# Another written-out issue order, with other banks and buffers, for attention followed by a gated FFN

## The chip, the cores and the metric

The kernel runs on one core of a Trainium2 chip. The metric is the device time of one execution in microseconds (us); the runs of one kernel are summed up by their median. The engines are called PE (TensorE), ACT (ScalarE), DVE (VectorE), POOL (GpSimd) and SP (SyncE, which only issues DMAs here).

## The reference

```python
k_proj = np.einsum('ks,bhsd->bhkd', E, k)
v_proj = np.einsum('ks,bhsd->bhkd', F, v)
scores = scale * np.matmul(q, k_proj.transpose(0, 1, 3, 2))
scores = scores - np.max(scores, axis=-1, keepdims=True)
attn = np.exp(scores)
attn = attn / (np.sum(attn, axis=-1, keepdims=True) + 1e-09)
x = np.matmul(attn, v_proj)            # then (B, H, S, D) -> (B*S, H*D)
gate = 1.0 / (1.0 + np.exp(-(x @ w_gate)))
out = (gate * (x @ w_val)) @ w_out
```

Attention has 8 batches, 8 heads, 1024 positions and 64 values to a head; E and F project the 1024 positions of K and V to 64. The FFN has 8192 tokens, 512 inputs, 1536 hidden values and 512 outputs. Inputs and output are float32; PE works in bf16.

## The kernel before

**The work.** A batch b goes through these stages. POOL loads K, V and q (`load_kv`, `load_q`, all through `load`, L559) and converts them to bf16 on the way. PE projects K and V (jobs `kv`). The projected K is transposed by a DMA of SP (`turnk`; on PE for batches 0 and 1), and so is q (`turnq`, `transpose_q`, L1491, DMA at L1494). A score job (`sc`) is four matmuls of 128 columns for 128 tokens and half of the heads. DVE takes the maximum (`top`) and subtracts it (`sub`; in some jobs PE subtracts, with the matrix `minus`), ACT takes the exponential (`exp`) into `pt`, which lies in the K half of the K and V buffer. SP transposes `pt` into `eT` (`turnp`, L1685, DMA at L1688). The products with V (`xo`, matmuls of 130 columns) give the sums too; DVE inverts them (`inv`), DVE or POOL divides (`div`, after a copy `ko` by ACT where POOL does it), and SP transposes the result into `xT` (`turnx`, L1748). Batch 0 is done by `first_batch`, with transposes on PE and its own job names (`pk`, `pv`, `tk`, `tq`, `xo0`, `tp`).

The FFN takes the 8192 tokens in 16 blocks of 512. Apart from the first block (`plain_steps`) and from the first and last output products (`o_plain`, jobs `Oplain`, 12 matmuls of 512 columns each), the products are made by a Strassen–Winograd scheme with seven products of halves instead of eight (`seven`, jobs `GA11`, `GS1`, `VS1`, `VA12`, `OA22` and so on, 4 to 6 matmuls of 256 columns each), with sums of the weights (`wsum`), of x and of the hidden values. ACT forms tanh(0.5 x) (`tanh`), and DVE forms (tanh + 1) times the value (`gate0`, L1067, and `hidden`, L1226); the factor 0.5 is applied when an output leaves PSUM. SP stores the output (`store`, L1309). While the FFN of batch p runs, the scores and products of batch p+1 and the loads and transposes of batch p+2 are placed between its matmuls.

**What sets the order.** The code makes 2923 jobs, each on one engine, numbered in the order in which the code creates them. The tuple `ORDER` (L159 to 315) names all of them once, in the order in which they are issued. `Scheduler.run` (L361) goes through it:

```python
assert sum(i >= 0 for i in ORDER) == len(self.jobs) and len(PLACES) == len(slots)
for s, p in zip(slots, PLACES):
    s.at = p
return [(lambda i=i: fill(-i)) if i < 0 else self.jobs[i].body for i in ORDER]
```

`Plan.emit` (L101) turns the list into one queue for each engine, which that engine works through in order. An instruction waits by semaphores for what it reads, and for the earlier users of what it overwrites; everything queued behind it on the engine waits too. So the place of a job in ORDER sets its place in its engine's queue only; what stands between two jobs of different engines tells how much work of the one engine lies between them. All loads but those of E and F are issued by POOL and all transposes and stores by SP, so ORDER sets the order of the DMAs as well.

A negative entry of ORDER is a filler (`busy`, L727): a matmul of the identity into bank 7, which keeps PE busy where its data is not there yet. −2 has 512 columns, −1 has 256. All fillers lie in the first hundred entries.

`PLACES` (L316 to 343) gives for each use of a PSUM bank one of 8 banks (`pF0` to `pF3`, `pA0` to `pA3`), and for each use of an SBUF scratch buffer one of 13 (two in the former place of E and F, the others in `spare`). Two uses of the same bank follow each other, with a wait where the first is not done.

**Numbers that come up later.** 0 to 15 are loads of weights and q, 30, 28, 31 and 29 transposes of q on PE, 38, 32, 58, 52 scores of batch 0 with what follows, 72, 79, 122, 125 its first `xo0` products, 128 to 183 the plain first block; 184 to 189 the loads of batch 1, 194 to 217 and 366, 367 weight sums and loads of `w_out`; 314 and 321 the projections of batch 1, 326 to 329 its `turnq`, 334 and 361 scores. Of `turnp`, 338, 347, 356, 365 are batch 1; 962, 971, 980, 989 batch 3; 1330 to 1357 batch 4; 1698 to 1725 batch 5; 2066 to 2093 batch 6. Of `turnx`, 391, 1013 and 2485; of `turnk`, 683, 1051, 1419. 424, 425; 1042, 1043; 1778, 1779 are pairs of q loads. The first readers of 338, 962, 980 and 1698 on PE are the `xo` jobs 368, 997, 1021 and 1733.

Of the kernel before, what the change touches and what calls it, by code (L numbers as in the profile page):

```python
# [153 lines left out]
class Job:  # L154
# [5 lines left out]
    16, -2, -2, -2, 17, 18, 0, 19, -2, -2, -2, -1, 28, 30, 29, 20, 3, 31, 21, -2, -2, -1, 22, 4, 38, 32, 1, 39,  # L160
    -2, -1, 23, 33, 2, 40, 24, 41, 9, -2, -2, 48, 25, 50, 42, 49, 5, 26, 34, 27, 51, 7, 35, 43, -2, -2, -1, 58,
    52, 8, 59, 46, 68, 36, 10, 60, 69, 61, 53, 6, 70, 37, -2, -1, 54, 11, 71, 62, 55, -2, -1, 44, 12, 75, 47,
    45, 14, 56, -2, -2, 72, 76, 15, 73, 63, 74, 13, 57, -2, -2, 66, 129, 77, 184, 64, 67, 135, 65, 78, 134, 189,
    79, 140, 80, 81, 194, 141, 128, 146, 188, 131, 136, 196, 148, 138, 142, 150, 195, 147, 144, 130, 143, 132,
    149, 197, 145, 137, 133, 84, 82, 366, 85, 157, 83, 198, 151, 86, 153, 87, 201, 92, 88, 102, 103, 93, 89,
    104, 156, 139, 160, 158, 94, 105, 152, 90, 95, 112, 96, 168, 91, 113, 106, 170, 172, 107, 154, 97, 114, 161,
    162, 108, 115, 180, 109, 116, 98, 182, 100, 110, 169, 117, 101, 174, 99, 181, 155, 122, 111, 171, 120, 123,
    173, 159, 124, 199, 163, 118, 121, 165, 119, 200, 183, 125, 218, 126, 127, 282, 367, 219, 210, 164, 190,
    283, 185, 203, 220, 191, 166, 187, 175, 284, 221, 234, 202, 186, 285, 298, 192, 193, 222, 299, 212, 321,
    167, 235, 223, 206, 236, 205, 322, 204, 225, 209, 323, 286, 237, 226, 300, 207, 324, 238, 301, 224, 325,  # L170
    211, 229, 239, 227, 266, 230, 250, 416, 267, 231, 251, 241, 213, 232, 287, 270, 254, 242, 417, 302, 255,
    252, 217, 303, 245, 418, 271, 257, 240, 246, 258, 273, 419, 253, 268, 274, 314, 243, 228, 269, 329, 256,
    315, 244, 247, 316, 272, 259, 328, 233, 289, 208, 317, 263, 216, 275, 261, 318, 326, 305, 264, 262, 279,
    306, 248, 277, 327, 265, 319, 280, 290, 176, 278, 320, 249, 177, 178, 281, 425, 361, 260, 179, 334, 352,
    309, 362, 444, 424, 335, 215, 336, 353, 337, 363, 330, 445, 339, 343, 331, 293, 447, 340, 294, 332, 344,
    333, 341, 364, 338, 214, 357, 345, 348, 450, 429, 354, 346, 349, 448, 355, 310, 449, 342, 358, 288, 347,
    350, 368, 375, 304, 276, 453, 369, 376, 552, 370, 377, 291, 371, 351, 451, 359, 356, 378, 292, 307, 380,
    360, 387, 558, 308, 454, 365, 559, 381, 388, 553, 382, 295, 560, 555, 455, 372, 554, 570, 389, 373, 390,
    384, 567, 374, 383, 385, 399, 379, 392, 386, 571, 393, 400, 557, 568, 401, 556, 394, 391, 311, 296, 569,
    395, 411, 396, 404, 312, 572, 297, 446, 402, 452, 412, 573, 313, 413, 428, 414, 408, 397, 405, 561, 574,  # L180
    398, 406, 409, 562, 403, 436, 407, 410, 576, 566, 437, 520, 564, 415, 577, 438, 521, 536, 456, 427, 439,
    537, 524, 575, 457, 522, 525, 540, 426, 565, 523, 538, 458, 539, 527, 563, 459, 440, 488, 578, 460, 489,
    423, 526, 442, 528, 579, 441, 421, 541, 529, 531, 492, 422, 532, 543, 530, 443, 580, 461, 533, 544, 581,
    420, 463, 493, 534, 462, 464, 490, 542, 465, 491, 472, 545, 467, 473, 469, 547, 495, 548, 476, 546, 549,
    477, 494, 470, 496, 479, 550, 468, 478, 480, 504, 497, 499, 481, 505, 474, 535, 787, 501, 508, 551, 483,
    509, 475, 690, 789, 511, 484, 485, 512, 510, 502, 500, 506, 486, 471, 706, 513, 466, 515, 430, 707, 487,
    498, 516, 691, 514, 503, 482, 694, 431, 517, 507, 695, 696, 786, 710, 432, 518, 697, 711, 433, 692, 790,
    698, 713, 434, 754, 699, 708, 582, 714, 519, 701, 693, 788, 703, 755, 717, 704, 702, 770, 435, 756, 718,
    674, 586, 771, 709, 758, 757, 590, 587, 604, 759, 774, 591, 772, 775, 792, 588, 705, 592, 761, 589, 617,
    773, 762, 793, 605, 595, 794, 765, 777, 606, 766, 801, 596, 593, 802, 778, 791, 594, 597, 607, 599, 722,  # L190
    600, 598, 608, 781, 584, 803, 601, 795, 583, 609, 806, 602, 618, 723, 807, 603, 782, 726, 808, 619, 613,
    724, 585, 727, 610, 677, 796, 620, 614, 611, 629, 810, 700, 615, 612, 712, 725, 760, 715, 616, 811, 630,
    763, 621, 631, 729, 812, 716, 626, 632, 641, 800, 738, 642, 627, 676, 622, 643, 719, 628, 739, 799, 638,
    623, 767, 720, 624, 634, 730, 740, 639, 635, 721, 644, 742, 636, 764, 646, 741, 625, 733, 743, 650, 640,
    776, 637, 647, 804, 768, 633, 648, 734, 779, 653, 797, 728, 769, 805, 654, 645, 651, 655, 652, 649, 783,
    809, 665, 658, 745, 798, 659, 731, 816, 660, 926, 746, 784, 735, 661, 666, 813, 785, 667, 662, 736, 749,
    888, 688, 737, 824, 686, 750, 744, 825, 814, 687, 889, 747, 689, 828, 663, 826, 815, 829, 892, 668, 780,
    827, 818, 890, 732, 817, 927, 656, 819, 893, 664, 904, 891, 895, 905, 831, 657, 751, 832, 840, 752, 896,
    669, 835, 841, 921, 908, 753, 899, 842, 748, 900, 844, 909, 920, 856, 836, 894, 922, 845, 911, 906, 857,
    925, 672, 897, 847, 912, 671, 858, 843, 848, 915, 898, 923, 670, 860, 916, 859, 851, 673, 820, 861, 872,  # L200
    907, 901, 928, 830, 852, 873, 929, 924, 862, 833, 930, 902, 863, 932, 935, 864, 910, 903, 675, 867, 934,
    874, 931, 936, 875, 938, 913, 933, 937, 876, 865, 917, 877, 837, 918, 868, 869, 822, 1058, 838, 879, 878,
    914, 880, 846, 870, 939, 919, 1059, 940, 849, 834, 941, 1155, 821, 853, 942, 883, 823, 866, 943, 1060, 680,
    850, 854, 881, 944, 681, 882, 1062, 884, 682, 885, 945, 1154, 839, 683, 1063, 947, 855, 1061, 1065, 886,
    679, 1064, 1066, 1158, 948, 684, 1067, 1122, 678, 871, 949, 1069, 1123, 1071, 887, 1070, 1074, 952, 1157,
    1124, 953, 1156, 1075, 1126, 685, 1159, 954, 1076, 1072, 946, 1078, 1077, 1125, 1160, 1043, 1079, 955, 1161,
    1127, 1042, 956, 958, 1162, 1081, 959, 963, 957, 967, 1129, 968, 1163, 1130, 964, 1164, 1073, 960, 1082,
    1169, 1165, 965, 961, 1080, 969, 966, 1085, 962, 1083, 972, 970, 976, 1133, 973, 1168, 951, 1138, 1134, 977,
    950, 1087, 1139, 971, 1170, 974, 1088, 1140, 975, 1142, 978, 1171, 1090, 1143, 1089, 1174, 1091, 1086, 981,
    1068, 1145, 1141, 997, 1175, 1146, 998, 982, 999, 990, 1149, 1176, 1000, 983, 1094, 979, 1092, 991, 1150,  # L210
    992, 980, 994, 1106, 1093, 995, 993, 985, 996, 1095, 1002, 1178, 1044, 1003, 1107, 986, 1167, 1009, 1179,
    1004, 1010, 987, 1011, 1128, 1001, 984, 1084, 1012, 1006, 988, 1097, 1007, 1180, 1108, 1008, 989, 1144,
    1098, 1005, 1131, 1021, 1018, 1110, 1109, 1166, 1096, 1013, 1022, 1147, 1101, 1023, 1111, 1135, 1019, 1099,
    1014, 1151, 1136, 1103, 1015, 1172, 1152, 1016, 1020, 1113, 1017, 1033, 1104, 1030, 1114, 1173, 1024, 1102,
    1026, 1256, 1177, 1025, 1117, 1257, 1034, 1054, 1181, 1027, 1055, 1028, 1182, 1031, 1184, 1137, 1057, 1046,
    1192, 1132, 1153, 1260, 1035, 1029, 1183, 1258, 1193, 1185, 1272, 1032, 1261, 1045, 1036, 1194, 1056, 1273,
    1196, 1195, 1208, 1037, 1259, 1263, 1209, 1274, 1112, 1197, 1186, 1275, 1276, 1187, 1105, 1115, 1199, 1198,
    1148, 1200, 1212, 1264, 1118, 1119, 1277, 1210, 1289, 1120, 1213, 1294, 1041, 1100, 1279, 1121, 1039, 1203,
    1201, 1215, 1038, 1188, 1224, 1216, 1040, 1205, 1189, 1204, 1293, 1267, 1206, 1295, 1225, 1211, 1280, 1219,
    1268, 1116, 1240, 1283, 1296, 1190, 1228, 1284, 1262, 1229, 1288, 1226, 1241, 1297, 1291, 1265, 1231, 1220,  # L220
# [1697 lines left out]
```

## Time and profile before

| | us |
|---|---|
| runs shown: 517.05, 517.59, 518.25; median | 517.59 |
| the profiled execution, its own time | 517.73 |
| its span (first to last instruction in the profile) | 515.9 |
| PE busy | 510.7 (99%), granted clock 1.0 |
| DVE busy | 438.5 (85%) |
| ACT busy | 371.5 (72%) |
| POOL busy | 171.4 (33%) |
| end of the last matmul | 513.3 |

The profile comes from one execution; its own time lies 0.14 us above the median. Times inside it count from the start of the span. A line of the timeline gives start, duration, engine, line of the kernel, operation, what is written and read, how many instructions were joined in the line, and in brackets how long the engine stood idle before it and who released it. Matmuls overlap, and a line's duration includes the way through the array: the time that a matmul costs is the distance to the next start. For a DMA, the timeline shows the issue on SP or POOL; the chain of waits and the list of DMA issues show how long it took to land.

### The profile page before, as it was taken

To read this page: it belongs to the slowest core of one execution; us is meant where nothing else is said; L and a number is where in the kernel's file an instruction comes from. 1 tells how busy PE (TensorE), PEld (TensorE's weight loads), DVE (VectorE), ACT (ScalarE), POOL (GpSimd) and SP (SyncE) were. 2 spreads that over 40 slices of the span, in tenths; PEclk is the share of its full clock that TensorE was granted. 3 is DMA by queue.
4 is the path that set the end of the run, shared out by engine and by line. 5 is a ranking of instruction groups with operands and counts; after the bars stand their busy time and mean duration, and the time that the engine had idled before them with its cause. 6 is when DMAs were issued, how large, how long until landed. Compare 5 with 4: busy or idle time off the path is not lost.

```text
span 515.9 us, 12160 instructions
## 1 busy us (share of the span) xinstructions
PE 510.7 (99%) x4724; PEld 424.5 (82%) x4727; DVE 438.5 (85%) x849; ACT 371.5 (72%) x714; POOL 171.4 (33%) x199
## 2 busy tenths in 40 slices
PE   8999999999999999999999999999999999999997
PEld 4556858879988888888888899888998899888884
DVE  6869999599988998879987899988998899877781
ACT  1557956789885797777878677885878678785841
POOL 9965014600634225230364014350164301503020
PEclk9999999999999999999999999999999999999999
DMA  9999999946939598962759859893279947320104
GB/s 154 197 198 207 185 165 195 182 75 142 185 104 187 121 170 157 177 101 66 148 148 184 144 104 180 179 183 80 60 128 185 196 83 160 107 62 19 66 2 163
DMA packets 140570, 71.58 MB, mean 139 GB/s; under 512 B 97248, under 2 KB 132320, under 8 KB 140512
## 3 DMA queue, kind: packets, MB, share of 16 engines
q0 software_dynamic: 35952, 29.89, 38.6%
q1 hardware_dynamic: 104560, 40.91, 36.8%
q8 instruction: 37, 0.61, 0.5%
q14 instruction: 21, 0.17, 0.1%
HBM read 60.29 MB, written 16.78 MB: 149 GB/s over the span
## 4 chain that ended last, share of the span: by engine, by line
PE 94%; DMA 3%; DVE 1%; ACT 1%; issue 0%; POOL 0%; POOLq 0%
PE pA L519 48%; PE pF L519 46%; DMA eT<-KVs 2%; DMA KVs<-in_k_dram 1%; DVE topf L1646 1%; ACT spare L533 0%; DVE pA L1673 0%; ACT KVs L533 0%; POOL KVs L560 0%; DVE hT L1067 0%; ACT EF L533 0%; DVE pF L1673 0%; ACT kpd L533 0%; ACT ost L533 0%; DVE wV L548 0%
## 5 line engine op out<-in xcount | busy, mean ns | idle before, releaser
L533 ACT ACTIVATE spare<-pF 128x512 f32<-128x512 f32 (+2 forms) x160 | 90.7, 578 | 39.2 <-PE pF L519 28.7
L533 ACT ACTIVATE spare<-pA 128x512 f32<-128x512 f32 (+2 forms) x157 | 88.7, 578 | 28.0 <-PE pA L519 19.3
L548 POOL TENSOR_TENSOR hT<-hT,hS 128x512 bf16<-128x512 bf16 x42 | 48.0, 1158 | 114.0 <-PE pF L519 48.8
L1226 DVE SCALAR_TENSOR_TENSOR hT<-spare,pA 128x512 bf16<-128x512 f32 x65 | 43.7, 678 | 10.2 <-PE pF L519 5.2
L1735 POOL TENSOR_TENSOR KVs<-spare,inv 128x384 bf16<-128x384 f32 (+1 forms) x44 | 33.2, 765 | 55.4 <-PE pF L519 27.8
L533 ACT ACTIVATE spare<-spare 128x512 f32<-128x512 f32 x77 | 47.6, 629 | 2.2 <-DVE spare L1157 2.2
L1157 DVE TENSOR_TENSOR spare<-pF,spare 128x512 f32<-128x512 f32 x63 | 42.7, 682 | 5.3 <-PE pF L519 3.9
L519 PE MATMUL pA<-wO,hT 128*128 128x256 bf16 (+1 forms) x323 | 44.6, 280 | 0.1
L519 PE MATMUL pF<-wO,hT 128*128 128x256 bf16 (+1 forms) x286 | 43.8, 294 | 0.1
L519 PE MATMUL pA<-xT,wV 128*128 128x256 bf16 (+1 forms) x236 | 39.0, 287 | 0.0
L1157 DVE TENSOR_TENSOR spare<-pA,spare 128x512 f32<-128x512 f32 x52 | 35.3, 681 | 4.0 <-PE pA L519 3.1
L1226 DVE SCALAR_TENSOR_TENSOR hT<-spare,pF 128x512 bf16<-128x512 f32 x51 | 34.5, 678 | 2.7 <-PE pF L519 2.2
L519 PEld LDWEIGHTS pA<-wO,hT 128*128 128x128 bf16 x324 | 31.4, 98 | 6.1 <-issue 0.2
L519 PEld LDWEIGHTS pF<-wO,hT 128*128 128x128 bf16 x288 | 27.9, 98 | 9.1 <-ACT ost L533 0.2
L519 PE MATMUL pF<-xT,wG 128*128 128x256 bf16 (+1 forms) x208 | 34.5, 287 | 0.0
L519 PE MATMUL pA<-xT,wG 128*128 128x256 bf16 (+1 forms) x200 | 31.8, 283 | 0.0
L560 POOL DMA_DIRECT2D Qb<-in_q_dram x18 | 14.0, 784 | 49.0 <-DMA kpD<-kpd 19.1
L519 PE MATMUL pA<-xS,tG 128*128 128x256 bf16 x200 | 30.0, 273 | 0.0
L548 POOL TENSOR_TENSOR xS<-xT,xS 128x512 bf16<-128x512 bf16 x14 | 16.4, 1172 | 38.3 <-DVE xS L548 20.9
L519 PE MATMUL pF<-xS,wG 128*128 128x256 bf16 x192 | 28.6, 273 | 0.0
L519 PE MATMUL pA<-xS,tV 128*128 128x256 bf16 x192 | 28.6, 273 | 0.0
L519 PE MATMUL pF<-xS,wV 128*128 128x256 bf16 x192 | 28.3, 273 | 0.0
(185 smaller groups left out, 1315.8 us busy)
## 6 DMA issues: line engine op xcount, KB each, us to landing
out_dram<-ost SPq DMA_DIRECT2D x63, 256.0 KB, 2.4
KVs<-in_v_dram POOLq DMA_DIRECT2D x15, 512.0 KB, 10.6
KVs<-in_k_dram POOLq DMA_DIRECT2D x14, 512.0 KB, 9.0
Qb<-in_q_dram POOLq DMA_DIRECT2D x14, 512.0 KB, 9.4
wO<-in_moe_w_out_dram POOLq DMA_DIRECT2D x2, 768.0 KB, 15.7
KVs<-in_k_dram POOLq DMA_DIRECT2D x4, 256.0 KB, 7.3
Qb<-in_q_dram POOLq DMA_DIRECT2D x4, 256.0 KB, 11.2
wV<-in_moe_w_val_dram POOLq DMA_DIRECT2D x4, 256.0 KB, 17.2
```

The costliest lines, as they stand in the source:

```text
L519: lambda e: e.matmul(o, lhsT, rhs, **kw),
L533: lambda e: e.activation(o, i, func, scale=scale),
L548: fn = lambda e: e.tensor_tensor(o, a, b, op)
L560: add("POOL", lambda e: e.dma_start(o, i), r=r, w=w, dma=sem, cost=0.78, nbytes=nbytes)
L1157: lambda e: e.tensor_tensor(PB(b)[:, :] if stay else BF(s), PB(b)[:, :], BF(s), ALU.add),
L1226: lambda e: e.scalar_tensor_tensor(o, y.rearrange("p (j c) -> p j c", j=2), 1.0, x.rearrange("p (j c) -> p j c", j=2), ALU.add, ALU.mult,),
L1646: lambda e: e.tensor_reduce((top if by_pe(b, t, y) else topf)[:, n : n + 8], PB(bk)[:, :].rearrange("p (n k) -> p n k", n=8), mybir.AxisLi ...
L1735: fn = lambda e: e.tensor_tensor(xto.rearrange("p (g h d) -> p h g d", g=2, h=H)[:, hh[0] : hh[1], :, :], o[:, :, 0:DH].rearrange("p (h g) ...
```

## The change

`ORDER` and `PLACES` are replaced. The jobs, their instructions and all other code are the same. ORDER has 2949 entries instead of 2948: one more filler of 512 columns (20 instead of 19; the 6 of 256 stay). Of the 906 entries of PLACES, 800 differ. In the diff, the first lines of both lists are shown, the lines around 338, around 962 to 1021 and around 1698, and the first line of PLACES.

```diff
 ORDER = (
-    16, -2, -2, -2, 17, 18, 0, 19, -2, -2, -2, -1, 28, 30, 29, 20, 3, 31, 21, -2, -2, -1, 22, 4, 38, 32, 1, 39,
-    -2, -1, 23, 33, 2, 40, 24, 41, 9, -2, -2, 48, 25, 50, 42, 49, 5, 26, 34, 27, 51, 7, 35, 43, -2, -2, -1, 58,
-    52, 8, 59, 46, 68, 36, 10, 60, 69, 61, 53, 6, 70, 37, -2, -1, 54, 11, 71, 62, 55, -2, -1, 44, 12, 75, 47,
-    45, 14, 56, -2, -2, 72, 76, 15, 73, 63, 74, 13, 57, -2, -2, 66, 129, 77, 184, 64, 67, 135, 65, 78, 134, 189,
-    79, 140, 80, 81, 194, 141, 128, 146, 188, 131, 136, 196, 148, 138, 142, 150, 195, 147, 144, 130, 143, 132,
...
-    306, 248, 277, 327, 265, 319, 280, 290, 176, 278, 320, 249, 177, 178, 281, 425, 361, 260, 179, 334, 352,
-    309, 362, 444, 424, 335, 215, 336, 353, 337, 363, 330, 445, 339, 343, 331, 293, 447, 340, 294, 332, 344,
-    333, 341, 364, 338, 214, 357, 345, 348, 450, 429, 354, 346, 349, 448, 355, 310, 449, 342, 358, 288, 347,
-    350, 368, 375, 304, 276, 453, 369, 376, 552, 370, 377, 291, 371, 351, 451, 359, 356, 378, 292, 307, 380,
...
-    1124, 953, 1156, 1075, 1126, 685, 1159, 954, 1076, 1072, 946, 1078, 1077, 1125, 1160, 1043, 1079, 955, 1161,
-    1127, 1042, 956, 958, 1162, 1081, 959, 963, 957, 967, 1129, 968, 1163, 1130, 964, 1164, 1073, 960, 1082,
-    1169, 1165, 965, 961, 1080, 969, 966, 1085, 962, 1083, 972, 970, 976, 1133, 973, 1168, 951, 1138, 1134, 977,
-    950, 1087, 1139, 971, 1170, 974, 1088, 1140, 975, 1142, 978, 1171, 1090, 1143, 1089, 1174, 1091, 1086, 981,
-    1068, 1145, 1141, 997, 1175, 1146, 998, 982, 999, 990, 1149, 1176, 1000, 983, 1094, 979, 1092, 991, 1150,
-    992, 980, 994, 1106, 1093, 995, 993, 985, 996, 1095, 1002, 1178, 1044, 1003, 1107, 986, 1167, 1009, 1179,
-    1004, 1010, 987, 1011, 1128, 1001, 984, 1084, 1012, 1006, 988, 1097, 1007, 1180, 1108, 1008, 989, 1144,
-    1098, 1005, 1131, 1021, 1018, 1110, 1109, 1166, 1096, 1013, 1022, 1147, 1101, 1023, 1111, 1135, 1019, 1099,
...
-    1863, 1899, 1710, 1693, 1900, 1822, 1711, 1874, 1701, 1901, 1865, 1808, 1875, 1694, 1905, 1904, 1695, 1779,
-    1866, 1876, 1696, 1702, 1703, 1826, 1877, 1697, 1878, 1906, 1704, 1827, 1698, 1804, 1712, 1828, 1907, 1713,
...
-    1715, 1824, 1870, 1721, 1864, 1820, 1912, 1783, 1881, 1825, 1914, 1882, 1722, 1716, 1733, 1726, 1915, 1734,
...
-    1748, 1913, 1846, 1903, 1844, 1835, 1749, 1847, 1880, 1872, 1849, 1778, 1883, 1757, 1839, 1902, 1758, 1837,
...
+    16, -2, -2, -2, 17, 18, 0, 19, -2, -2, -2, -1, 30, 28, 31, 20, 1, 29, 21, -2, -2, -1, 22, 4, 38, 3, 32, 39,
+    -2, -1, 23, 2, 33, 40, 24, 5, 41, -2, 34, 48, 25, 50, 8, 42, 49, 26, 7, 27, 51, 35, 43, -2, -2, -2, -1, 58,
+    6, 59, -2, -1, 46, 9, 52, 47, 68, 36, 10, 60, 69, 53, 61, 11, 37, 70, -2, 54, 75, 12, 55, 62, 44, 71, 13,
+    45, 56, 14, -2, -2, -2, -1, 72, 76, 74, 15, 63, 73, 57, -2, -2, 66, 129, 77, 64, 67, 135, 65, 78, 134, 79,
+    147, 80, 81, 194, 146, 140, 128, 142, 196, 141, 144, 143, 195, 136, 130, 131, 132, 197, 148, 133, 149, 150,
...
+    262, 319, 306, 216, 326, 249, 176, 320, 280, 177, 265, 278, 425, 178, 334, 281, 289, 309, 179, 361, 335,
+    352, 424, 343, 444, 336, 214, 337, 362, 290, 353, 363, 330, 445, 339, 293, 331, 447, 294, 340, 260, 332,
+    344, 333, 215, 338, 341, 348, 448, 450, 345, 342, 446, 349, 346, 310, 364, 347, 350, 276, 304, 451, 288,
+    354, 351, 357, 368, 375, 358, 355, 453, 369, 376, 356, 552, 370, 377, 291, 378, 429, 307, 292, 371, 359,
...
+    1126, 1075, 1124, 954, 945, 955, 1076, 887, 946, 1078, 1125, 956, 1160, 950, 1043, 1079, 953, 1067, 963,
+    957, 1161, 1042, 964, 1127, 958, 1077, 1071, 1162, 1129, 965, 967, 1130, 1163, 959, 1081, 1072, 1164, 968,
+    1082, 972, 966, 960, 1167, 1169, 1073, 969, 1133, 1168, 1080, 973, 961, 1138, 1083, 970, 976, 962, 1170,
+    974, 1139, 1087, 977, 975, 971, 1142, 1088, 1171, 1140, 1068, 1085, 978, 1134, 981, 1089, 1174, 1143, 1141,
+    1090, 997, 1175, 1091, 998, 1086, 999, 1145, 979, 982, 990, 1000, 1106, 1146, 980, 994, 983, 1092, 1176,
+    1149, 995, 991, 992, 1178, 951, 1150, 984, 993, 1094, 1093, 996, 985, 1095, 1002, 1009, 986, 1179, 1001,
+    1107, 1010, 1003, 1097, 987, 1004, 1128, 1084, 988, 1006, 1108, 1007, 1011, 1110, 989, 1098, 1008, 1012,
+    1021, 1144, 1180, 1131, 1096, 1005, 1111, 1022, 1109, 1172, 1023, 1147, 1014, 1024, 1013, 1018, 1113, 1019,
...
+    1893, 1817, 1859, 1895, 1801, 1420, 1685, 1860, 1802, 1894, 1680, 1689, 1421, 1688, 1623, 1778, 1805, 1861,
+    1690, 1708, 1779, 1806, 1691, 1800, 1818, 1896, 1692, 1681, 1709, 1693, 1821, 1803, 1897, 1822, 1807, 1898,
...
+    1703, 1904, 1865, 1700, 1876, 1697, 1826, 1701, 1809, 1698, 1905, 1877, 1702, 1712, 1704, 1878, 1827, 1906,
+    1713, 1866, 1816, 1705, 1907, 1828, 1819, 1706, 1869, 1714, 1829, 1830, 1707, 1733, 1879, 1823, 1820, 1715,
...
 PLACES = (
-    0, 3, 4, 2, 1, 2, 6, 1, 5, 0, 2, 0, 0, 1, 4, 3, 3, 2, 5, 0, 1, 0, 2, 1, 1, 5, 5, 0, 0, 8, 1, 10, 4, 2, 4, 2,
...
+    0, 3, 4, 2, 2, 1, 6, 1, 5, 0, 4, 4, 0, 1, 0, 3, 3, 2, 5, 4, 1, 1, 4, 2, 2, 5, 5, 2, 2, 8, 0, 9, 3, 7, 5, 7,
...
```

318 rows, old and new, of tables (ORDER, PLACES) are left out of this document.

## The prediction

> **What bounds the kernel now.** I read the page from its top: busy shares, the chain that ended last, then PE by stages, then the waits of PE, and at each wait the timeline around it.
>
> ```profile
> PE 510.7 (99%) x4724; PEld 424.5 (82%) x4727; DVE 438.5 (85%) x849; ACT 371.5 (72%) x714; POOL 171.4 (33%) x199
> ...
> q8 instruction: 37, 0.61, 0.5%
> ...
> PE 94%; DMA 3%; DVE 1%; ACT 1%; issue 0%; POOL 0%; POOLq 0%
> ```
>
> PE is busy 99% of the span and is 94% of the chain. Busy does not prove full speed, so I look at the step of a matmul. The chain has runs of PE work with nothing between:
>
> ```profile
> 57.56 1.31 PE pA L519 x12
> ```
>
> 12 matmuls of 256 columns in 1.31 us is 109 ns each; in the same way 512 columns take 216 ns, 130 columns 59, 128 columns 56. Priced with these steps, all PE work from the first K projection (7.50 us) on is 499.6 us. The work is fixed, so the list can win only what PE stands still between 7.50 and its last matmul (513.3 us). The stages show where that is:
>
> ```profile
> core 0: us, PE busy (x) PEld busy (x) DVE busy (x) ACT busy (x) POOL busy (x), PEclk, DMA share, GB/s
> 0.00:22.00 22.00, 19.93 (x163) 10.22 (x163) 16.27 (x51) 7.58 (x14) 20.87 (x32) 1.00 1.18 172
> ...
> 65.92:200.00 134.08, 133.61 (x1257) 112.87 (x1258) 120.09 (x233) 100.85 (x197) 44.18 (x50) 1.00 0.84 153
> 200.00:350.00 150.00, 150.00 (x1434) 132.17 (x1432) 131.62 (x250) 116.10 (x224) 50.26 (x57) 1.00 0.80 147
> ```
>
> The granted clock is 1.00 throughout. After 22 us almost nothing is left. Going through PE's rows and subtracting the step of each matmul from the distance to the next, I find 1.66 us of standing after 22 us that another order could remove: 0.16 at 22.6, and some 1.5 after 66 us. The two largest are these:
>
> ```profile
> 72.66 1.23 SPq L1688 DMA_TRANSPOSE eT<-KVs  x1
> ...
> 74.00 1.91 SPq L1494 DMA_TRANSPOSE qT<-Qb  x1
> ...
> 76.34 0.60 PE L519 MATMUL pA<-xS,wG 128*128 128x256 bf16 x4
> ...
> 77.14 0.35 PE L519 MATMUL pF<-vpD,eT 128*128 128x130 bf16 x3 [0.19 <-DMA eT<-KVs]
> ```
>
> Four steps of 109 ns from 76.34 end at 76.78; the `xo` product (job 368) starts at 77.14, so PE stood 0.36 us. It waited for the transpose of exponentials that SP issued at 72.66 (job 338). The chain shows how long that and a later one (980) took:
>
> ```profile
> 72.66 4.43 DMA eT<-KVs
> ...
> 191.90 4.82 DMA eT<-KVs
> ```
>
> The reader of 980 (job 1021) came 0.34 us late. The reader of 962 (997) came 0.07 us late, behind a transpose of 5.58 us. About 0.7 us is in pieces of 0.04 to 0.17 us behind ACT and DVE. So at most 1.6 us (0.3%) can be won; nothing bounds a loss.
>
> **What a transpose needs.** All 90 transposes of SP have an issue and a landing in the trace. The 59 with no load from POOL and no packet of PE's instruction fetch (queue q8, 37 of them, one for about 250 PE instructions, 12 to 13 us apart, 0.96 us each) beside them take 3.0 to 3.75 us, median 3.20. The 26 with such a fetch beside them have a median of 4.2, the 5 with a load alone 4.49; 18 of 90 are over 4.0. Against that stands what I call the cover: the PE work that ORDER lists between a transpose and its first reader. An issue comes 0.39 us ahead of its listed place in the median (5th percentile 1.2 ahead, 95th 0.48 behind). A reader waits, then, by about (duration − 0.39 − cover), where positive.
>
> **The change, part by part.** The same instructions stand in another order, with other banks and buffers, and one more filler of 512 columns on PE.
>
> *Start, to 22 us.* The weight loads are issued in another order. I lined up the new PE queue with the measured durations: the first `sub` product keeps 18.82, the ten products after it and the fillers follow without a gap, and the first `xo0` product that before had at 24.18 would start at 23.83, 0.35 us earlier; the 0.16 at 22.6 goes, one filler (0.216) is added. Every weight in my line-up lands at least 0.5 us ahead of its use.
>
> *The wall at 62 to 66 us.* The first scores of batch 1 need q transposed:
>
> ```profile
> 59.61 6.46 SPq L1494 DMA_TRANSPOSE qT<-Qb  x4
> ...
> 65.92 0.39 PE L519 MATMUL pF<-kpD,qT 128*128 128x128 bf16 x4
> ```
>
> The last q load ends a queue of loads that never runs dry from 21 to 62 us (2.5 us for each 512 KB). The new list puts the same bytes ahead of it, so I keep its landings: the two transposes needed first land at 63.4 and 65.3. Before, the reader came 0.60 us after that. In the new list the first reader (334) has 0.22 us less PE work ahead of it (54.64 instead of 54.86, fillers counted), and the start does this work 0.57 sooner (0.35 earlier, with 0.216 of filler more behind it): 65.92 − 0.22 − 0.57 = 65.13, so it waits to 65.35. Work after it is 445.16 us instead of 444.73. From before's 65.92 + 444.73 = 510.65 to 65.35 + 445.16 = 510.51: **−0.14** is all that the start leaves. Bounds: −0.35 if q lands earlier; +0.5 if the loads end 0.6 us later (a quarter of one 512 KB load).
>
> *338.* Cover 3.48 (two scores 0.45, an output product 2.59, one Strassen product 0.44) becomes 3.91 (one Strassen product more). Also 424, a q load beside it, is listed 2.4 us of PE work earlier. At 4.43 the wait would shrink by 0.43, more than its 0.36; a fetch near it leaves some chance of a longer one. **−0.30**, bounds −0.36 and +0.3.
>
> *980.* Cover 4.37 becomes 5.24, so 4.82 fits: **−0.34**, bounds −0.34 and 0.
>
> *962.* Cover 5.04 becomes 3.72: two scores and two products now stand ahead of it. The q loads 1043 and 1042 are listed where they were (167.5 and 168.4 us of PE work; before 167.8 and 168.4) and landed, before, at 172.9 and 176.4 on the same scale; 962 is listed at 173.9, so most of it still lies beside the second one. By the median with a load, 4.49 − 0.39 − 3.72 = 0.38, and its 0.07 of before goes: **+0.31**; bounds −0.07 (at 3.2) and +1.40 (at the 5.58 of before).
>
> *1698 and the short covers.* The new list has 14 transposes with cover under 4.0 (338, 347, 356, 391, 683, 962, 1013, 1051, 1357, 1348, 1419, 1698, 2075, 2485; least 3.05 and 3.28), the old list 8. At 3.2 none of them waits. 1698 (3.72) has two q loads moved ahead of it (listed 8.3 and 7.4 us before it; a q load lands 6 to 9 us after issue): **+0.10**, bounds 0 and 0.4. I place the fetches by the number of PE instructions, as in the trace; of the other twelve only 338 and 347 stand near one. So they get 0; the bound is the rival below.
>
> *Waits on ACT and DVE.* By PE distance 78 readers had under 0.3 us of margin and 76 have it now; under 1 us 358 and 340. **0**, bounds −0.5 and +0.5.
>
> *Ending.* After the last matmul one copy and one store, 2.6 us, in both; the last jobs lined up show no gap: **0**.
>
> Sum: −0.14 − 0.30 − 0.34 + 0.31 + 0.10 = −0.37. The profiled execution took 517.73 (span 515.9); 517.73 − 0.37 = 517.36. It lies 0.14 above the median of 517.59, so the forecast is **517.2**.
>
> **Rivals.**
> (a) *Nearly all waits go.* Start as above (−0.14), 338, 980 and 962 without wait (−0.36, −0.34, −0.07) and the pieces behind ACT and DVE too (some −0.7): −1.5, with 1698's +0.10 kept −1.4: **516.2**. For it: each wait can be removed by distance alone. Against it: the counts of narrow margins hardly fall.
>
> (b) *Covers decide nothing.* If what makes a transpose long is not its neighbours in time but happens to the ones that PE waits for, moves give and cost nothing: only the −0.14 stays, **517.45**. Against: 3.20 without neighbours, 4.2 and 4.49 with them. The Trainium skill, "Runtime: NRT & Kernel Launch", section "Instruction fetch mechanics", says that instructions are refilled in blocks of 256 and that crossing such a border is "mostly hidden". Its block agrees with a fetch for about 250 instructions here; for PE's own queue no row shows a stop at a fetch, but the transposes beside one are 1 us longer, which that sentence does not mention; by it, the transposes near a fetch would need no more cover than others and this rival's time would hold.
>
> (c) *The short covers run late; slower.* If the 14 lie beside a load, a store or a fetch more often than I place them, each waits by its duration − 0.39 − cover. At 4.2 their sum is 1.8 us, at 4.49 about 5.4; the old list's covers give 1.3 and 3.5 in the same way. The first three parts win 0.78; the lateness passes that and the 0.2% bound (1.03) together from 1.8 us on: 962's 0.31 and three more at 0.5 (a transpose of some 4.6). With four more at 0.5: 2.31 − 0.78 = +1.5 on the median, **519.1**. For it: 18 of 90 were over 4.0, which is 2.8 of 14 if my placing of fetches says nothing.
>
> (d) That the list does other work than before is excluded: same instructions but one filler.
>
> **How the numbers follow.** What can be told from no change is 0.2%, 1.03 us: faster is below 516.56, slower above 518.62. Forecast 0.42 (516.7 to 518.1), (a) 0.20, (b) 0.10, (c) 0.28. Faster 0.20 is (a); same 0.52 is the forecast with (b); slower 0.28 is (c). The range runs from (a) to a little over (c): 516.2 to 519.3, with a tenth left out at each end.
>
> **What would show it.** Right: no gap on PE ahead of 368 and 1021, one of 0.3 to 0.4 ahead of 997; the first scores of batch 1 start near 65.4; sum of PE's standing after 66 us 1.2 to 1.6. Wrong: scores later than 66 us (loads late, the wall moves everything), or several gaps of 0.3 to 1 ahead of `xo` products and of the first product of a block (readers of transposes), which is (c); or gaps of over 0.2 behind ACT and DVE, of which I expected none new.

## The result, and the profile after

| | before | after |
|---|---|---|
| median of 9 runs each | 517.59 | 519.42 |
| lowest and highest run | 516.98 to 519.26 | 518.62 to 520.38 |
| the profiled execution, its own time | 517.73 | 520.38 |
| its span | 515.9 | 518.6 |

The ratio is 1.0034, with a 95% interval of 1.0022 to 1.0047: the change makes the kernel slower by 1.83 us (0.34%). The profiled execution of after is the slowest of its nine runs, 0.96 above their median; so its trace shows where the time went, but more of it than the median has.

Page, parts 1 and 4, of after:

```profile
PE 510.4 (98%) x4725; PEld 424.3 (82%) x4728; DVE 438.6 (85%) x849; ACT 372.5 (72%) x714; POOL 170.6 (33%) x199
...
PE 93%; DMA 4%; DVE 2%; ACT 1%; issue 0%; POOL 0%; POOLq 0%
```

PE is busy as long as before, in a span that is 2.7 us longer. The work is the same; PE stands still more. The same stages as before show where (length, then busy time of PE, PEld, DVE, ACT, POOL, clock, DMA share, GB/s):

```profile
65.92:200.00 134.08, 132.93 (x1248) 112.38 (x1249) 118.07 (x231) 101.40 (x197) 41.41 (x50) 1.00 0.86 149
200.00:350.00 150.00, 148.28 (x1417) 130.18 (x1415) 129.91 (x246) 113.42 (x219) 51.30 (x58) 1.00 0.75 145
```

In the second stage before had no idle time of PE; after has 1.72 us. In the first it was 0.47 and is 1.15. The long transposes of the chain of waits are now three:

```profile
72.78 4.70 DMA eT<-KVs
...
185.27 5.10 DMA eT<-KVs
...
307.48 5.14 DMA eT<-KVs
```

They are 338, 962 and 1698. 980, long before, took 3.07. The timeline of PE at the readers of the last two, 997 and 1733:

```profile
188.96 0.61 PE L519 MATMUL pA<-xT,wG 128*128 128x256 bf16 x4
190.41 0.29 PE L519 MATMUL pA<-vpD,eT 128*128 128x130 bf16 x2 [0.84 <-DMA eT<-KVs]
...
310.90 0.60 PE L519 MATMUL pF<-xS,tG 128*128 128x256 bf16 x4
312.67 0.29 PE L519 MATMUL pF<-vpD,eT 128*128 128x130 bf16 x2 [1.16 <-DMA eT<-KVs]
```

Four steps of 109 ns after 188.96 end at 189.40, and 997 starts at 190.41: 1.01 us late. For 1733 it is 312.67 − 311.34 = 1.33. To see why the transposes landed late, look at what POOL had under way. The timeline of POOL, and the landings of its two loads of q (1043 and 1042) from issue, in us:

```profile
178.96 1.52 POOL L560 DMA_DIRECT2D Qb<-in_q_dram  x2 [13.98 <-DMA qT<-Qb]
...
DMA to landing us min/median/max: 6.9/8.0/9.0
```

The second load, issued at 179.74, lands at 188.74, and 962, issued at 185.27, at 190.37: 1.63 us after the load. 1698 was issued at 307.48, 7.5 us after the load 1779, which landed at 309.72; two stores ahead of 1698 in SP's queue landed at 310.13 and 310.78, and 1698 at 312.62.

The third loss is on DVE. Timelines of DVE, POOL and PE:

```profile
341.38 1.37 DVE L548 TENSOR_TENSOR xS<-xT 128x512 bf16<-128x512 bf16 x1
...
341.27 1.21 POOL L548 TENSOR_TENSOR hT<-hT,hS 128x512 bf16<-128x512 bf16 x1 [0.28 <-PE pF L519]
...
343.42 0.39 PE L519 MATMUL pF<-xS,wG 128*128 128x256 bf16 x2 [0.56 <-DVE spare L1157]
```

The sum 1924 on DVE (0.42 us in the trace of before) began 0.11 us after a sum of POOL (2035) and took 1.37, until 0.27 us after POOL's end. The sum `plusG` 1969 behind it came late, and the product 1973 that waits for it started 0.72 us late.

### The profile page after: what moved, and what is told of

Its sections match the earlier page's. It is cut to its first block, busy times and chain, and to the rows that moved or that the text cites. A ratio compares the mean times of both kernels' runs of the same rounds, so it can differ in the third digit from the quotient of the medians.

```text
span 518.6 us, 12152 instructions
## 1 busy us (share of the span) xinstructions
PE 510.4 (98%) x4725; PEld 424.3 (82%) x4728; DVE 438.6 (85%) x849; ACT 372.5 (72%) x714; POOL 170.6 (33%) x199
## 4 chain that ended last, share of the span: by engine, by line
PE 93%; DMA 4%; DVE 2%; ACT 1%; issue 0%; POOL 0%; POOLq 0%
PE pA L519 49%; PE pF L519 44%; DMA eT<-KVs 3%; DMA KVs<-in_k_dram 1%; DVE topf L1646 1%; DVE xS L548 0%; DVE pA L1673 0%; ACT KVs L533 0%; POOL KVs L560 0%; ACT ost L533 0%; DVE pF L1673 0%; DVE hT L1067 0%; ACT spare L533 0%; DVE spare L1157 0%; ACT EF L533 0%
## 5 line engine op out<-in xcount | busy, mean ns | idle before, releaser
L1735 POOL TENSOR_TENSOR KVs<-spare,inv 128x256 bf16<-128x256 f32 (+1 forms) x49 | 34.5, 715 | 84.3 <-ACT spare L533 25.2
L519 PE MATMUL pA<-wO,hT 128*128 128x256 bf16 (+1 forms) x383 | 55.3, 286 | 0.1
L1226 DVE SCALAR_TENSOR_TENSOR hT<-spare,pF 128x512 bf16<-128x512 f32 x65 | 43.6, 678 | 8.6 <-PE pF L519 6.5
L519 PE MATMUL pF<-xT,wV 128*128 128x256 bf16 (+1 forms) x244 | 38.9, 281 | 0.1
L1226 DVE SCALAR_TENSOR_TENSOR hT<-spare,pA 128x512 bf16<-128x512 f32 x48 | 32.4, 678 | 3.4 <-PE pA L519 2.3
L519 PE MATMUL pA<-wT,hS 128*128 128x256 bf16 x252 | 33.7, 273 | 0.0
L519 PE MATMUL pF<-wO,hT 128*128 128x256 bf16 (+1 forms) x226 | 32.9, 288 | 0.1
L519 PE MATMUL pF<-xS,tV 128*128 128x256 bf16 x216 | 32.4, 273 | 0.0
L519 PE MATMUL pA<-wT,hT 128*128 128x256 bf16 x240 | 31.7, 273 | 0.0
L533 ACT ACTIVATE EF<-pA 128x512 f32<-128x512 f32 (+2 forms) x33 | 18.7, 574 | 15.8 <-PE pA L519 14.3
```

The costliest lines, as they stand in the source:

```text
L519: lambda e: e.matmul(o, lhsT, rhs, **kw),
L533: lambda e: e.activation(o, i, func, scale=scale),
L1226: lambda e: e.scalar_tensor_tensor(o, y.rearrange("p (j c) -> p j c", j=2), 1.0, x.rearrange("p (j c) -> p j c", j=2), ALU.add, ALU.mult,),
L1735: fn = lambda e: e.tensor_tensor(xto.rearrange("p (g h d) -> p h g d", g=2, h=H)[:, hh[0] : hh[1], :, :], o[:, :, 0:DH].rearrange("p (h g) ...
```

## The experiments

Two theories were set against each other. **L:** a transpose beside a load of q is long, and the new list has taken the cover away at two such places. **F:** the long transposes come from their place, by PE's instruction fetch or SP's own queue. A third (D) was that the loss is spread over ACT and DVE. Each time is set against the kernel before, measured again beside each group of four: 517.54, 517.60 and 517.82. The changed kernel is +1.83 in these terms; the 95% intervals of these differences reach 0.5 to 1.1 us to each side. Only ORDER is edited unless it is said otherwise, so the diffs show only the entries that move, with a neighbour or two (in e4, 1046, 1045 and 1044 also leave their old places).

**Loads later: e1_q4_later, e2_q5_later, e3_all_later, e4_before_q_later**

```diff
@@ e1
-    950, 1043, 1079, 953, 1067, 963, 957, 1161, 1042, 964,
+    950, 1079, 953, 1067, 963, 957, 1161, 964,
...
-    1185, 1184, 1054,
+    1185, 1184, 1043, 1042, 1054,
...
-    1173, 1045, 1020,
+    1173, 1020,
...
-    1263, 1044, 1200,
+    1263, 1045, 1044, 1200,
@@ e2
-    1688, 1623, 1778, 1805, 1861, 1690, 1708, 1779, 1806,
+    1688, 1623, 1805, 1861, 1690, 1708, 1806,
...
-    1920, 1839, 1847, 1780, 1872,
+    1920, 1778, 1779, 1839, 1847, 1872,
...
-    1848, 1781, 1750,
+    1848, 1750,
...
-    1761, 1940,
+    1761, 1780, 1781, 1940,
@@ e3: the moves of e1, e2 and e6, and
-    352, 424, 343,
+    352, 343,
...
-    391, 400,
+    391, 424, 400,
...
-    412, 427, 313,
+    412, 313,
...
-    415, 438,
+    415, 427, 438,
@@ e4, in the list of before
-    1160, 1043, 1079,
+    1160, 1079,
...
-    1161, 1127, 1042, 956,
+    1161, 1127, 956,
...
-    1025, 1117,
+    1025, 1043, 1042, 1117,
...
-    1037, 1259,
+    1037, 1046, 1045, 1044, 1259,
...
-    444, 424, 335,
+    444, 335,
...
-    391, 311,
+    391, 424, 311,
```

Expected:

> The changed kernel, with the two q loads 1043 and 1042 listed behind the stores 1184 and 1185 (some 23 us of PE work later), so that they lie beside no transpose of batch 3's exponentials; the q transpose 1045 moves behind them. Theory L (a q load beside a transpose makes it long, and the cover of 3.72 us is then too short): transpose 962 takes 3.0 to 3.7 us instead of 5.10, the gap of 1.01 us ahead of its reader 997 goes, and the time falls by about 1.0 to 518.4. Theory F (the long transpose comes from its place: the instruction fetch or SP's own queue): 962 stays at 4.5 to 5, the time stays at 519.4. Theory D (the loss is spread over waits on ACT and DVE and differs from run to run): the gap may go, the time falls by under 0.4.

> The changed kernel, with the q loads 1778 and 1779 listed behind the store 1920 (some 22 us of PE work later) and the q transposes 1780 and 1781 behind transpose 1761. Theory L: transpose 1698 takes 3.0 to 3.7 us instead of 5.14, the gap of 1.33 us ahead of its reader 1733 goes, and the time falls by about 1.3 to 518.1. Theory F: 1698 stays near 5 and the time at 519.4. Theory D: the time falls by under 0.4.

> The changed kernel with both pairs of q loads moved as in the first two, the q load 424 listed behind transpose 391 (so not beside 338), and the DVE sum 1924 listed behind 1974, so that it doesn't run beside POOL's sum 2035. Theory L: no gap ahead of 368, 997, 1733; the gap of 0.72 us ahead of 1973 goes too; the profiled sum of these four is 3.4 us, so 516.0 to 517.0. Theory F: only the 0.7 ahead of 1973 goes, 518.7. Theory D: about 519.

> The kernel before, with 1043, 1042 listed behind transpose 1025, their q transposes 1046, 1045, 1044 behind 1037, and the load 424 behind transpose 391 (427 and 426 are behind that already). Theory L: 338 takes 3.0 to 3.7 instead of 4.43, 962 and 980 the same instead of 5.58 and 4.82; the gaps of 0.36, 0.07 and 0.34 ahead of 368, 997 and 1021 go, so 0.8 less than the kernel before: 516.8. Theory F: the three gaps stay, 517.6.

Measured: 524.79 (+7.25), 519.99 (+2.45), 531.44 (+13.90) and 528.54 (+11.00). As bids for a faster kernel all four fail, and none of the four forecasts of the time holds. But the two gaps went (in e3 all four that it was made against). In e1, 962 took 3.56 us and PE ran on (timeline of PE, e1):

```profile
188.62 0.61 PE L519 MATMUL pA<-xT,wG 128*128 128x256 bf16 x4
189.06 0.28 PE L519 MATMUL pA<-vpD,eT 128*128 128x130 bf16 x2
```

In e2, 1698 took 3.64 and the gap ahead of 1733 went. That speaks against F at these two. In e4 only 962 became short (3.65); 338 and 980 stayed long with no load beside them, 4.33 and 4.61 us, and PE waited 0.25 and 0.14 for them. Beside each lay one packet of the instruction fetch (queue q8). The chain of waits at 338, and the DMA queues from its issue to its landing, without a packet of POOL's queue q0 (e4):

```profile
72.11 4.33 DMA eT<-KVs
```

```profile
q1 hardware_dynamic: 1569, 0.39, 87.3%
q8 instruction: 1, 0.02, 2.1%
```

So at 338 and 980 theory L fails, and F, with the fetch for the place, fits. The time was lost where the loads went instead. In e1 (chain of waits, then waits of PE):

```profile
202.54 13.07 DMA xT<-KVs
...
220.06 11.75 DMA KVs<-in_k_dram
```

```profile
PE pF L519 <- DMA KVs<-in_k_dram: 3.1, 2, 2.9
```

The transpose 1025, issued at 202.54, 0.01 us before the second load (202.55 to 215.29) and 0.79 after the first, took 13.07 us and landed 0.32 after the second. The loads of K and V wait for the transposes of that buffer, so they came late too, and PE stood for them. In e2 the new victim was 1749 (5.30 us, though issued 0.60 ahead of the first load; 3.11 in the change), whose reader 1928 came 1.33 late; in e3 and e4 it was also 391, behind 424 (8.2 us in e4; PE stood 3.2 to 4.3 us). None of the places tried for a load of q was free: each time something that SP issued beside it was late.

**Loads sooner, DVE apart, more cover: e5_q4_sooner, e6_dve_apart, e7_more_cover, e8_three_mended**

```diff
@@ e5
-    947, 1159, 683, 1061,
+    947, 1159, 678, 683, 1061,
...
-    685, 678, 1074,
+    685, 1074,
@@ e6
-    2019, 1924, 2038, 2035, 1969, 2005, 1980, 2006, 1973, 1774, 1981, 2162, 1974, 1944,
+    2019, 2038, 2035, 1969, 2005, 1980, 2006, 1973, 1774, 1981, 2162, 1974, 1924, 1944,
@@ e7
-    1090, 997, 1175, 1091, 998, 1086, 999, 1145, 979, 982, 990, 1000, 1106,
+    1090, 1175, 997, 1091, 998, 1086, 999, 1145, 979, 982, 1000, 1106, 990,
...
-    1707, 1733, 1879, 1823, 1820, 1715, 1910, 1734,
+    1707, 1879, 1823, 1820, 1715, 1910, 1733, 1734,
@@ e8: the moves of e5 and e6, and 1733 as in e7
```

> The changed kernel with only the q transpose 678 listed ahead of the transpose 683 of projected K instead of behind it. The loads 1043 and 1042 are then released by 683 (174.8 us) instead of by 678 (178.3), some 3.5 us sooner, and land at about 182.4 and 185.2 instead of 185.9 and 188.7, ahead of the issue of transpose 962 at 185.3. Theory L (a transpose lands 1 to 2 us after the load that it lies beside): 962 takes 3.0 to 3.7 us, the gap of 1.01 us ahead of 997 goes, no load is later than before: 518.4. Theory F (place on SP or the fetch): 962 stays at 5 and the time at 519.4.

> The changed kernel with only the DVE sum 1924 listed behind the DVE job 1974, so that it doesn't begin beside POOL's sum 2035. Theory P (a bf16 sum of DVE that begins beside a tensor operation of POOL is held until that ends: 1.37 us instead of 0.42): plusG 1969 comes about 1 us sooner, the gap of 0.72 us ahead of 1973 goes, 518.7 if it is there in every run. Theory C (the gap is a chance of the profiled execution): under 0.3 less.

> The changed kernel with its loads as they are and more PE work ahead of two readers: product 997 behind 1175 (0.66 us more; 990, which uses the same bank, behind 1106) and product 1733 behind 1910 (1.09 us more). Theory L: the transposes 962 and 1698 stay at 5.1 us each, and the gaps shrink by the added cover, 1.01 to about 0.35 and 1.33 to about 0.25: 1.7 less, 517.7. A theory by which the loss is not at these two readers but moves with the whole schedule: 519.4.

> The changed kernel with 678 ahead of 683, 1733 behind 1910 and 1924 behind 1974. Theory L and P: the gaps of 1.01, 1.33 and 0.72 us become 0, 0.25 and 0: 2.8 less, 516.6, which is 1.0 below the kernel before. If the gains don't add, 517.6 or more.

e5: 521.35 (+3.75). 962 took 3.49 and its gap went, as L has it, but the loads now lay beside the stores 950 and 953, which took 6.7 and 7.0 us instead of 2.0 and 2.4. The next copy into their buffer (1168) waited for them, and PE for that copy (timeline of PE, e5):

```profile
186.22 0.50 PE L519 MATMUL pF<-xT,wV 128*128 128x256 bf16 x3 [1.52 <-ACT ost L533]
```

e6: 518.71 (+1.11), 0.72 less than the change. The moved sum took 0.41 us, and no gap was left ahead of 1973 (timeline of DVE, e6):

```profile
342.63 0.41 DVE L548 TENSOR_TENSOR xS<-xT 128x512 bf16<-128x512 bf16 x1
```

The gap stands at 0.72 in all seven traces of the changed list that leave 1924 in place, so it is no chance: theory P holds and C falls.

e7: 518.51 (+0.91), 0.92 less than the change, where 1.7 was expected. 962 still took 4.9 and 1698 5.3; the gaps fell to 0.14 and 0.43. But a gap of 0.58 came up ahead of 1106 (timeline of PE, e7):

```profile
191.01 0.39 PE L519 MATMUL pF<-xT,wV 128*128 128x256 bf16 x2 [0.41 <-DVE hT L1226]
```

The inverse 998, now waiting for the later 997, held the DVE job 1086 behind it in its queue. e8, the sum of the three mends, gave 521.35 (+3.75): the stores of e5 again, with a gap of 3.78 us in the profiled execution.

**The rest: e9_cover_dve, e10_no_q_loads, e11_before_q5_pair, e12_less_filler**

```diff
@@ e9: the moves of e6 and e7, and
-    1091, 998, 1086, 999,
+    1091, 1086, 998, 999,
@@ e10, in load_q (ORDER as in the change)
         def load_q(b, R, after=()):
+            if b in (4, 6):
+                return
@@ e11, in the list of before
-    1849, 1778, 1883,
+    1849, 1883,
...
+    1779, 1778, 1866,
@@ e12
-    14, -2, -2, -2, -1, 72,
+    14, -2, -2, -1, 72,
```

> The changed kernel with 1924 behind 1974, product 1733 behind 1910, product 997 behind 1175 with its inverse 998 behind the DVE job 1086 (in the run before, 998 ahead of 1086 held DVE until 997 was done, 0.58 us of PE) and 990 behind 1106. Theory L with P: 0.71 for 1924 as measured, about 0.9 each for the two readers: 517.0, below the kernel before (517.6). If the new gap of 0.58 stays: 517.6.

> The changed kernel without the q loads of batches 4 and 6 (four loads of 512 KB: 1042, 1043, 1778, 1779), so that these batches work on the q of an earlier batch; all else is issued as it was. Theory L: 962 and 1698 take 3.0 to 3.7 us, their gaps go: 1.0 plus what 1698 costs in the median run (0.5 to 1.3), 517.1 to 517.9. Theory F (place, fetch): 962 and 1698 stay long, 519.4.

> The kernel before, with the q load 1778 listed right behind 1779 as in the changed kernel, so that two loads stand ahead of 1698 (cover 5.69 here) instead of one. Theory Q (a transpose lands 1 to 2 us after the load that was issued ahead of it): the second load lands near 315, 1698 near 316 instead of 312.8, its reader 1733 (314.5) waits 1 to 2 us: 518.6 to 519.6. Theory S (a load adds 1 to 2 us to a transpose, however long the load goes on): 1698 takes 4.5 to 5.6, lands by 314, no gap: 517.6.

> The changed kernel with one of the three fillers of 512 columns ahead of job 72 left out, so 19 as in the kernel before. If the extra filler costs its 0.216 us: 519.2. If job 72 waits there for the copy 45 anyway (it landed at 20.50, 72 began at 20.73) and the first block for ACT: 519.4, no change.

e10: 517.98 (+0.16), 1.67 less than the change. Without the four loads 962 and 1698 took 3.56 and 3.60, with the same place, queue and cover, and both gaps were gone (timeline of PE at 997, e10):

```profile
188.71 0.61 PE L519 MATMUL pA<-xT,wG 128*128 128x256 bf16 x4
189.16 0.28 PE L519 MATMUL pA<-vpD,eT 128*128 128x130 bf16 x2
```

F falls for these two. The gap of 0.72 ahead of 1973 was still there: with e6's 0.72 the two causes together are 2.4 us, more than the 1.83 lost; the difference lies within the intervals, and the change has a gain as well (980).

e11 tells how a load lengthens a transpose. In the list of before, with a cover of 5.69 us at 1698, a second load behind the first gave 521.38 (+3.56). The landings of the two loads and of 1698 and 1707, in us from issue, and PE at their readers (e11):

```profile
DMA to landing us min/median/max: 5.7/7.1/8.5
```

```profile
DMA to landing us min/median/max: 7.6/7.7/7.7
```

```profile
315.68 0.29 PE L519 MATMUL pA<-vpD,eT 128*128 128x130 bf16 x2 [1.27 <-DMA eT<-KVs]
...
318.76 0.35 PE L519 MATMUL pF<-vpD,eT 128*128 128x130 bf16 x3 [1.35 <-DMA eT<-KVs]
```

The second load landed at 314.87, 1698 at 315.64 and 1707 at 318.71; PE stood 1.43 and 1.51 us. That is theory Q, and more than its 1 to 2 us, as a second transpose is caught. A load adds no fixed time (theory S): 1698 took 7.64 us and landed behind the second load, however long that went on.

e12: 519.61 (+1.79). The two forecasts lie only 0.2 apart, too little for these medians, but the trace tells them apart: without the filler, job 72 began at 20.74 us (20.73 in the change) and job 79 at 24.12 (24.13), so the extra filler costs nothing.

e9: 517.68 (−0.14 against 517.82; ratio 1.000, 0.9991 to 1.0009). It puts both readers farther from their transposes and the sum apart from POOL's, and takes back all of the loss, though 962 still took 4.74 us and 1698 4.40. PE's idle time from 66 to 513 us is 0.14 us (windows, e9):

```profile
65.92:200.00 134.08, 133.94 (x1261) 113.21 (x1259) 119.12 (x233) 102.11 (x199) 42.61 (x51) 1.00 0.87 151
200.00:350.00 150.00, 150.00 (x1434) 131.83 (x1433) 130.55 (x248) 115.36 (x223) 50.25 (x57) 1.00 0.78 147
350.00:513.00 163.00, 163.00 (x1514) 140.03 (x1511) 133.85 (x247) 114.85 (x220) 37.97 (x41) 1.00 0.45 101
```

0.6 us better than the kernel before was expected, from e6 and the two readers; the 0.14 lies within the interval. No version was found that beats the kernel before.

## Why the prediction was wrong

The forecast of 517.2 lies within 0.2% of before, and the change is slower by 0.34%, outside the range by 0.1 us. Rival (c) named the side, the price (519.1) and two of the places. By steps, in the profiled execution of after against that of before:

| step | predicted | measured | |
|---|---|---|---|
| start and wall | −0.14 | −0.05 | held |
| 338 | −0.30 | +0.01 | see below |
| 980 | −0.34 | −0.34 | held |
| 962 | +0.31 | +0.94 | mis-sized |
| 1698 | +0.10 | +1.33 | mis-sized |
| waits on ACT and DVE | 0 | +0.72 and under 0.1 | failed |
| ending | 0 | 0 | held |
| sum | −0.37 | +2.6 | 2.65 by the two own times |

*Start and wall.* The PE work done by 70 us is 0.27 us ahead of before, the filler counted; without its 0.216 that is 0.05. The wall was not reached: the second q transpose landed at 64.22 instead of 65.31, and the first score started at 65.42 without a gap. The landings that I had kept moved, to the good side, but PE arrived later than I had it: the first block waited 0.23 us for ACT at 22.53, and job 79 started at 24.13, not at 23.83.

*338.* It took 4.70 beside the load 424, which landed at 76.57, 0.91 us before the transpose did. In the nine experiments on the changed list that left its load in place, the gap ahead of 368 was gone (338 took 3.15 to 4.13 us there). But it was gone in e11 too, on the list of before (3.95). The term was read off one execution on each side, and what it is worth in the median stays open.

*980* held, with room to spare: its reader came 5.61 us after the issue, so 4.82 would have fitted. That it took only 3.07 was not foreseen. The instruction fetch, which began 2.6 us after its issue in before, began 3.9 after it here, when the transpose had landed. (The fetches of before lie 9.0 to 17.8 us apart, not the 12 to 13 that I read.)

*962 and 1698* are the step that failed. I named both, with their covers and loads, and then priced 962 by a duration, the median of five transposes beside a load, 4.49 (it took 5.10), and 1698 at 0.10, with its loads to land 6 to 9 us after issue (the second took 9.74, and 1698 took 5.14). The rows of before show a rule that I had not drawn from them. Twelve issues of SP after 66 us had a load ahead of them with at least 0.5 us still to go, and every one landed after that load, 0.77 to 3.97 us later; in the trace of after it is fifteen, 0.41 to 2.90. (In the twelve experiments it is 166 of 176; the ten that landed ahead are all stores.) For a transpose the landing of the load is what counts, and the cover has to reach beyond it. Even so, with the loads where before's trace had them, this rule would not have given the loss: 962 would wait some 0.3 us (load 1042 at 176.4 on the scale of PE work, the transpose 1.49 later as in before, the reader at 173.9 + 3.72), and 1698 0 to 0.4 (load 1.2 us after the listed place, the transpose 1.5 to 2.9 later, the reader at 3.72). The loads themselves took longer, 9.0 and 9.7 us from issue instead of 8.6, and 1698 stood behind two late stores as well. In other executions with the same cover 1733's gap was 0.43 to 1.33 (0.47 in e6, 1.25 in e12); this and 368's 0.36 are probably why the median lost 0.8 less than the profiled execution.

*ACT and DVE.* Counting narrow margins said that nothing would change, and nothing of that kind did. What came was no narrow margin but a single operation that took 0.95 us longer beside POOL; my margins used each operation's duration from before. The trace of before had three such sums too (1.07, 1.37 and 1.68 us), off PE's path. e6 shows the price: 0.72.

*Rivals.* (a) fell: waits went at 980, and came elsewhere; its own terms add up to −1.61, not −1.5. (b) fell by e10 and e7: time beside a load and cover each decide. (c) was right in kind, and its condition (962 and three or four more at some 4.6 us) too broad: it took two at 5.1, and the sum on DVE for the rest.

The Trainium skill, "DMA: Bandwidth & Descriptors", section "Queues, rings and completion order", says that each DMA engine takes turns between the queues that have work, one packet at a time. The traces agree, by the packets that the profile counts, where both queues have some to move: 343 of the load's queue and 345 of SP's in 3 us (last section). Counted in packets a transpose is larger than a load, so turns don't bring it through first.

## What to carry to other kernels

Price a transfer of many small packets beside a load by the load's landing, not by a mean duration: list every transfer issued while a load is in flight, and see whether its reader is far enough for load and transfer together. Look at the instruction fetch in the same way. A load that is moved takes its shadow along, on stores and transposes alike, and the next loads wait for those. When readers move, look at what stands behind the inverse or copy that waits for them; and keep sums of DVE from starting beside sums of POOL where PE waits for what is queued behind.

## What the runs showed of the hardware

In all six places where PE had stood still for 3.1 to 4.3 us (e1, e3, e4, e8) the granted clock was then 0.5 for 3.4 us (6.8 in e1), which I had not counted in moving the loads. Windows of e4, around the gap ahead of 520 (the column behind POOL is the granted clock):

```profile
89.50:92.70 3.20, 0.15 (x3) 0.04 (x2) 0.00 (x1) 0.00 (x0) 1.11 (x1) 1.00 1.18 285
92.70:96.00 3.30, 3.30 (x16) 2.31 (x17) 2.25 (x5) 1.21 (x3) 1.91 (x2) 0.50 1.26 176
96.00:100.00 4.00, 4.00 (x38) 3.53 (x36) 1.67 (x4) 3.34 (x7) 3.36 (x5) 0.99 0.96 176
```

A matmul of 256 columns took about 213 ns instead of 109 there, so a wait of 3.2 us cost about 4.9 (1.7 for the 16 matmuls). Gaps of 1.0 to 1.7 us, as in the change or in e5, had no such after-effect.

Part of why a load holds back a transpose stands in the packets of the two queues (q0 has POOL's loads, q1 what SP issues; the numbers are packets, MB and share of the engines' time). In the traces a load of q moves as 512 packets of 1024 bytes, a transpose as 1024 of 256, a store as 128 of 2048. While both queues have work, their packets go one for one, so the load is through before the transpose; a store, with 128, need not wait so long, which fits the ten. DMA queues of after from 144 to 147 us, with the load 675 and the transpose 677 (8.00 us from issue to landing):

```profile
q0 software_dynamic: 343, 0.35, 86.4%
q1 hardware_dynamic: 345, 0.09, 33.5%
```

That is not all. In e11, in the 4.3 us from the issue of 1698 behind two loads, its queue moved one packet (308.00 to 312.30):

```profile
q0 software_dynamic: 725, 0.73, 113.5%
...
q1 hardware_dynamic: 1, 0.00, 0.0%
```

And 1749 in e2 landed 2.7 us after its last packet began, with loads behind it; in after it was 0.5. Why the first packet and the landing come so late there, no run here shows.
